# Loads of x in an FFT-mixing and ELU kernel: two-row loads cut in halves, gather lists one a step, the channel matrix in front

## The chip, the cores and the metric

The kernel runs on one core of one Trainium2 chip. The metric is the device time of one execution in microseconds (us), the median of several runs. Five engines work side by side: TensorE (PE; its weight loads are PEld), VectorE (DVE), ScalarE (ACT), GpSimd (POOL) and SyncE (SP), whose queue issues most DMA transfers. The transfers themselves run on 16 DMA engines that all queues share.

## The reference

`x` is 8 batches of 3008 rows and 256 channels. The kernel takes the real part of a 2-D Fourier transform of each batch (along the rows and along the channels) and sends every row through a two-layer network with ELU in between:

```python
def _attn_ref(x):                         # x: (8, 3008, 256) float32
    X = np.fft.fft(x, axis=1)
    X = np.fft.fft(X, axis=2)
    return X.real.astype(np.float32)

def _moe_ref(x, w_in, w_out):             # (24064, 256), (256, 2048), (2048, 256)
    h = x @ w_in
    g = np.where(h > 0.0, h, 1.0 * (np.exp(np.minimum(h, 0.0)) - 1.0))
    return (g @ w_out).astype(np.float32)
```

The weights come as float64, and the kernel converts them itself.

## The kernel before

The transform along the rows uses the symmetries of cosine and sine. The rows of a batch are loaded as four tiles L[0] to L[3] (named `xl` in the profile), two in ascending order (0 and 3, plain loads on the sync queue) and two in descending order (1 and 2, gathers on the GpSimd queue, with row numbers from a small table `ix`). Each partition of a tile holds four rows of one part of the sequence and two rows of another. The tiles are folded (sums e, differences o, then E, O, EO), and the folded tiles are multiplied by the matrices MC. The transform along the channels is folded into the first weight matrix: `fold_chunk` multiplies a converted chunk of `w_in` by the channel matrix CC and gives Wc and Ws.

The loads of one batch:

```python
    def load_x(b):
        L = [
            spool.tile([128, 6 * ND], FP, tag=f"xl{j}", bufs=1, name=f"xl{j}")
            for j in range(4)
        ]
        for j in (2, 1):
            for c, cols in (
                (2 if j == 1 and b == NB - 1 else 0, slice(2 * ND, 6 * ND)),
                (1, slice(0, 2 * ND)),
            ):
                load = nc.gpsimd.indirect_dma_start(
                    out=L[j][:, cols], out_offset=None, in_=xflat,
                    in_offset=bass.IndirectOffsetOnAxis(
                        ap=ix[:, c : c + 1].bitcast(U32), axis=0),
                    element_offset=(b * SEQ + (HALF if j == 1 else 0)) * ND,
                )
                if b == 1:
                    pin(load)
        for j, row in ((3, HALF), (0, 0)):
            nc.sync.dma_start(out=L[j][:, 0 : 4 * ND], in_=xrows(b, row, 4, 128, 4))
            nc.sync.dma_start(
                out=L[j][:, 4 * ND :],
                in_=bass.AP(
                    tensor=xt,
                    offset=x.offset + (b * SEQ + row + 512) * ND,
                    ap=[[2 * ND, 2], [4 * ND, 64], [1, 2 * ND]],
                ),
            )
        ...                                     # one short row of the last batch
        return L
```

`pin` keeps an instruction in program order; instructions without it are placed by a scheduler, which may move them ahead once their tiles are free. `ap` lists step and count of each dimension of the source, slowest first.

The start of the program:

```python
    for _ in range(46):                         # warm-up matmuls on zeros
        mm(idle, zero, zero[:, 0:1].to_broadcast([128, 512]), True)
    exp_neg(warm)
    w1_chunks[0].load()
    L_first = load_x(0)
    nc.sync.dma_start(out=CC, in_=CC_dr.ap())
    load_mats(0, 0, (BE,))
    w1_chunks[1].load()
    nc.sync.dma_start(out=pick, in_=PK_dr.ap())
    ...
    at(-25.0, lambda: fold_now("e3 c3"))        # VectorE folds of the first batch
    at(-24.9, w1_chunks[0].scale)
    at(-24.8, lambda: fold_now("o3 e2 c2 E2 o2 O2"))
    at(-24.5, begin_x_even)                     # xa, xg, xd, xe: read all of L[0..3]
    at(-24.4, lambda: fold_now("e0 c0 e1 c1 E0 EO0"))
    ...
    at(-13.2, lambda: fold_chunk(0))            # first matmuls after the warm-up
    at(-13.1, lambda: dft_now(state["x_even"], 0, "pC"))
    at(-13.0, lambda: dft_now(R_even, 0, "pA"))
```

Everything after that is laid out in steps of `T = 4.8` units of schedule time, 47 steps to a batch. In a step VectorE and ScalarE make the ELU of one block, GpSimd forms four sums of its parts G (for a Strassen-like product) and TensorE multiplies. From batch 2 on GpSimd also folds the next batch's x, one piece in most steps, in 39 of the 47. The loads of the next batch are called once, eight steps before its batch begins:

```python
    for b in range(1, NB):
        s0 = (b - 1) * steps_b
        late = 2 if b == 1 else 0
        l0 = s0 - 8 if b > 1 else 3.2
        at(l0 * T + 0.1, lambda b=b: state.update(L=load_x(b)))
        ...
        def fold_slot(n):
            if b > 1:
                return s0 - 1 + 39 * n // n_big
```

Of the kernel before, what the change touches and what calls it, by code (L numbers as in the profile page):

```python
# [17 lines left out]
SEQ = 3008  # L18
ND = 256
NDFF = 2048  # L20
NF = NDFF // 128
HALF = SEQ // 2
# [85 lines left out]
def kernel(  # L108
# [7 lines left out]
    nc = tc.nc  # L116
    NB = x.shape[0]
# [18 lines left out]
    pin = tc.keep_in_program_order  # L136

    xt = x.tensor

    def xrows(b, row, step, n, rows=6):  # L140

        return bass.AP(
            tensor=xt,
            offset=x.offset + (b * SEQ + row) * ND,
            ap=[[step * ND, n], [1, rows * ND]],
        )
# [23 lines left out]
            )  # L170

    def load_x(b):
        L = [
            spool.tile([128, 6 * ND], FP, tag=f"xl{j}", bufs=1, name=f"xl{j}")
            for j in range(4)
        ]
        for j in (2, 1):
            for c, cols in (
                (2 if j == 1 and b == NB - 1 else 0, slice(2 * ND, 6 * ND)),
                (1, slice(0, 2 * ND)),  # L180
            ):
                load = nc.gpsimd.indirect_dma_start(  # L182
                    out=L[j][:, cols],
                    out_offset=None,
                    in_=xflat,
                    in_offset=bass.IndirectOffsetOnAxis(
                        ap=ix[:, c : c + 1].bitcast(U32), axis=0
                    ),
                    element_offset=(b * SEQ + (HALF if j == 1 else 0)) * ND,
                )  # L190
                if b == 1:
                    pin(load)
        for j, row in ((3, HALF), (0, 0)):
            nc.sync.dma_start(out=L[j][:, 0 : 4 * ND], in_=xrows(b, row, 4, 128, 4))
            nc.sync.dma_start(
                out=L[j][:, 4 * ND :],
                in_=bass.AP(
                    tensor=xt,
                    offset=x.offset + (b * SEQ + row + 512) * ND,
                    ap=[[2 * ND, 2], [4 * ND, 64], [1, 2 * ND]],  # L200
                ),
            )
        if b == NB - 1:
            nc.gpsimd.dma_start(
                out=L[1][0:1, 2 * ND : 5 * ND], in_=xrows(b, SEQ - 3, 1, 1, 3)
            )
        return L


    CC = cpool.tile([128, 384], FP, tag="CC")  # L210
# [10 lines left out]
    class Chunk:  # L221
# [7 lines left out]
        def load(self):  # L229
            dst = self.dst()  # L230
            home = self.home
            if isinstance(home, tuple) and (wide or self.pairs):
                tag, bufs, size = home
                home = spool.tile([128, size], FP, tag=tag, bufs=bufs, name="raw")
            self.ab = home[:, 0:512]
            if not wide:
                nc.sync.dma_start(out=dst, in_=self.src)
                return
            words = home[:, 0:1024].bitcast(I32)
            self.raw = words.rearrange("p (n w) -> p n w", w=2)  # L240
            n = dst.shape[1]
            nc.sync.dma_start(
                out=words.rearrange("p (a b) -> p a b", a=n), in_=self.src.bitcast(I32)
            )
# [137 lines left out]
    def load_mats(ri, kodd, cuts=()):  # L382
        n = (2 * ri + kodd) * BW
        ends = (0, *cuts, BW)
        for a, z in zip(ends, ends[1:]):
            nc.sync.dma_start(
                out=MC[ri, kodd][:, a:z], in_=MC_dr.ap()[:, n + a : n + z]
            )
# [112 lines left out]

    def fold_x(L, engine_of, pieces):

# [254 lines left out]
    def spread_ext(b, kodd):  # L758
        for sl, a, z in ring_cut(b * HALF + kodd * RUN, RUN, False):
            a, z = a + kodd * RUN, z + kodd * RUN  # L760
            nc.sync.dma_start(
                out=Rb[:, sl],
                in_=r128_dr[b : b + 1, a:z].to_broadcast([128, z - a]),
            )
            nc.sync.dma_start(out=Ir[127:128, sl], in_=r128_dr[b : b + 1, a:z])
# [332 lines left out]
    state = {}  # L1098
# [2 lines left out]
        mm(idle, zero, zero[:, 0:1].to_broadcast([128, 512]), True)  # L1101
    exp_neg(warm)
    w1_chunks[0].load()
    L_first = load_x(0)
    nc.sync.dma_start(out=CC, in_=CC_dr.ap())  # L1105
    load_mats(0, 0, (BE,))
    w1_chunks[1].load()
    nc.sync.dma_start(out=pick, in_=PK_dr.ap())
# [16 lines left out]
    def at(t, fn):  # L1125
        events.append((t, len(events), fn))
# [52 lines left out]
    T = PERIOD  # L1179
    for chunk, k in (  # L1180
# [15 lines left out]
        t = k * T  # L1196
# [18 lines left out]
    for c in range(1, 8):  # L1215
        at((2 * c - 2) * T + 4.7 if c > 1 else 2.3, lambda c=c: fold_chunk(c))
        t = (2 * c - 1) * T + 0.03 if c > 1 else 3.0
# [19 lines left out]
    for slot in range(total):  # L1237
        i = slot % 2 * 8 + slot // 2 if slot < 16 else slot
        t = slot * T
# [45 lines left out]
    for q in range(2, n_tiles):  # L1285
        t = (8 * q + 9) * T
# [14 lines left out]
    def safe(col):  # L1301

        return 8 * ((col - 1 - RING) // TW) + 8 if col > RING else 0
# [17 lines left out]
    def at_dft(step, gap, b, ri, kodd, stat):  # L1321
        box = []

        def d():
            if not box:
                box.append(Dft(ri, b, kodd, stat()))
            return box[0]

        at_half(step, d, 0, 0)
        at_half(step + gap, d, 1, b * HALF + (kodd + 1) * RUN)  # L1330

    def begin_folds(b):
        state["EO"], state["ops"] = fold_x(state["L"], lambda key: nc.gpsimd, 2)
# [22 lines left out]
    for n in range(16):  # L1356
        j, k = divmod(n, 4)
# [15 lines left out]
    for b in range(1, NB):  # L1373
        s0 = (b - 1) * steps_b
        late = 2 if b == 1 else 0
        l0 = s0 - 8 if b > 1 else 3.2
        at(l0 * T + 0.1, lambda b=b: state.update(L=load_x(b)))
        first = (6, 7, 7, 8, 9, 9, 10, 10, 12, 15)

        def fold_slot(n):  # L1380
            if b > 1:
                return s0 - 1 + 39 * n // n_big
            return first[n] if n < len(first) else 17 + n - len(first)

        at(fold_slot(0) * T, lambda b=b: begin_folds(b))
        n = 0
        for key in fold_keys:
            slot = fold_slot(n)
            at(
                slot * T + (3.5 if slot < 16 else 1.3),  # L1390
                lambda key=key: state["ops"][key](),
            )
            n += key[0][0] not in "cx"
        for n, (ri, kodd) in enumerate(((0, 0), (1, 0), (0, 1), (1, 1))):
            at_dft(
                s0 + (28, 34 + late, 38 + late, 42 + late)[n], 2, b, ri, kodd,
                lambda k=2 * ri + kodd: state["EO"][k],
            )
        for kodd in range(2):
            step = s0 + (35 if late else 28, 38 + late)[kodd]  # L1400
            assert step >= safe(b * HALF + (kodd + 1) * RUN)
            at(step * T + 1.0, lambda b=b, kodd=kodd: spread_ext(b, kodd))
# [50 lines left out]
```

## Time and profile before

| | |
|---|---|
| time, median of 3 runs | 1982.79 us (1981.92 to 1983.54) |
| span of the profiled execution | 1980.7 us |
| busy: TensorE, GpSimd, VectorE, ScalarE | 1940.8, 1379.1, 1296.3, 864.8 us |
| moved by DMA | 70.25 MB, mean 35 GB/s; 289 GB/s in the first fortieth of the span |
| gathers of x (DMA_INDIRECT on GpSimd) | 32, median 958 ns each on the engine |
| sums of G on GpSimd | 1440, mean 728 ns |
| two-row loads of x | 16, 256 KB each |

In the profile, L414 is the line of all matmuls, L423 that of all GpSimd sums, L182 that of the gathers, L194 and L195 the plain loads of x, L1105 the load of CC. A group is written as line, engine, operation, out<-in. "PE H L414 <- DVE xg L420" reads: a matmul into H waited for VectorE's xg.

### The profile page before, as it was taken

The numbers are of one execution on the slowest core, as the hardware profiler recorded it, in microseconds if no ns is written. First come the engines' busy times: TensorE is split into PE (matmuls) and PEld (weight loads), VectorE is DVE, ScalarE is ACT, GpSimd is POOL, SyncE is SP. The second block draws the span as 40 slices with busy tenths as digits, with TensorE's granted clock in tenths as the row PEclk, the third lists the DMA queues.
The fourth block names the chain that finished last, engine by engine and source line by source line (L and its number), as shares of the span: only waits on it lengthen the run. The fifth ranks groups of instructions, "written<-read, shape, count | busy, mean of one in ns | idle before, by whom it ended". The sixth has DMA issues, their size and how long they took to land.

```text
span 1980.7 us, 27003 instructions
## 1 busy us (share of the span) xinstructions
PE 1940.8 (98%) x8912; PEld 1651.8 (83%) x8912; DVE 1296.3 (65%) x2393; ACT 864.8 (44%) x1669; POOL 1379.1 (70%) x1821
## 2 busy tenths in 40 slices
PE   7999999999999999999999999999999999999998
PEld 4788788888888888888888888888888888888887
DVE  6976666666666666666666666666666666666666
ACT  2654434444344444444444443444444444344443
POOL 2788767786587865777667775678757777455665
PEclk8999999999999999999999999999999999999999
DMA  8235210121011110011101211002010010100101
GB/s 289 80 21 49 60 25 15 36 64 19 13 17 46 48 28 15 18 43 45 27 13 19 59 29 29 11 19 77 18 22 12 19 20 15 18 12 11 22 9 24
DMA packets 263130, 70.25 MB, mean 35 GB/s; under 512 B 248446, under 2 KB 249362, under 8 KB 262992
## 3 DMA queue, kind: packets, MB, share of 16 engines
q1 hardware_dynamic: 257200, 55.69, 14.7%
q0 software_dynamic: 3616, 12.59, 2.0%
q8 instruction: 70, 1.15, 0.3%
q14 instruction: 68, 0.56, 0.1%
q10 hardware_dynamic: 2176, 0.26, 0.1%
HBM read 43.66 MB, written 24.80 MB: 35 GB/s over the span
## 4 chain that ended last, share of the span: by engine, by line
PE 89%; POOL 5%; DVE 3%; issue 1%; SPq 1%; ACT 1%; DMA 0%; DVEq 0%; POOLq 0%; ACTq 0%
PE H L414 36%; PE pB L414 15%; PE pD L414 15%; PE pC L414 15%; PE pA L414 7%; POOL G L423 2%; POOL xl L182 1%; POOL WT L423 1%; DVE E L810 1%; POOL w L423 1%; SPq L1105 0%; DVE G L836 0%; DMA raw<-in_moe_w_in_dram 0%; DVE pow L314 0%; DVE v L420 0%
## 5 line engine op out<-in xcount | busy, mean ns | idle before, releaser
L423 POOL TENSOR_TENSOR G<-G 128x256 f32<-128x256 f32 x1440 | 1034.7, 728 | 528.3 <-DVE G L836 350.4
L810 DVE SCALAR_TENSOR_TENSOR E<-Rb,wex,H 128x256 f32<-128x256 f32 x752 | 328.0, 478 | 582.6 <-PE H L414 577.9
L426 ACT ACTIVATE G<-H 128x512 f32<-128x512 f32 x376 | 224.5, 597 | 974.3 <-DVE G L820 963.7
L414 PE MATMUL H<-Ir,Ws 128*128 128x256 f32 x1504 | 387.1, 380 | 2.7 <-DVE E L810 1.7
L414 PE MATMUL H<-Rr,Wc 128*128 128x256 f32 x1504 | 387.0, 380 | 0.0
L414 PE MATMUL pC<-G,WT 128*128 128x256 f32 x1440 | 369.6, 379 | 1.6 <-DVE u L420 1.6
L414 PEld LDWEIGHTS H<-Rr,Wc 128*128 128x128 f32 x1504 | 284.6, 190 | 56.0 <-issue 3.4
L414 PEld LDWEIGHTS H<-Ir,Ws 128*128 128x128 f32 x1504 | 277.5, 189 | 52.2 <-DVE E L810 4.9
L414 PEld LDWEIGHTS pC<-G,WT 128*128 128x128 f32 x1440 | 273.5, 190 | 39.1 <-issue 2.0
L820 DVE SCALAR_TENSOR_TENSOR G<-E,H 128x512 f32<-128x512 f32 x376 | 256.9, 683 | 48.2 <-POOL G L423 15.2
L836 DVE SCALAR_TENSOR_TENSOR G<-G,H 128x512 f32<-128x512 f32 x376 | 255.7, 680 | 21.6 <-ACT G L426 21.5
L836 DVE SCALAR_TENSOR_TENSOR G<-M,G 128x512 f32<-128x512 f32 x376 | 256.8, 683 | 0.0
L426 ACT ACTIVATE G<-G 128x512 f32<-128x512 f32 x376 | 233.2, 620 | 0.0
L414 PE MATMUL pA<-G,w 128*128 128x256 f32 x784 | 229.3, 379 | 0.6 <-DVE bs L420 0.6
L414 PE MATMUL pD<-G,w 128*128 128x256 f32 x784 | 229.3, 379 | 0.0
L414 PE MATMUL pB<-G,w 128*128 128x256 f32 x784 | 229.3, 379 | 0.0
L414 PE MATMUL pB<-G,WT 128*128 128x256 f32 x720 | 215.7, 381 | 10.4 <-POOL G L423 10.3
L426 ACT ACTIVATE M<-G 128x512 f32<-128x512 f32 x376 | 224.3, 596 | 0.0
L426 ACT ACTIVATE M<-M 128x512 f32<-128x512 f32 x376 | 220.9, 588 | 0.0
L414 PE MATMUL pD<-G,WT 128*128 128x256 f32 x720 | 214.7, 380 | 2.9 <-DVE v L420 2.5
L414 PEld LDWEIGHTS pA<-G,w 128*128 128x128 f32 x784 | 148.9, 190 | 21.1 <-issue 0.9
L414 PEld LDWEIGHTS pD<-G,w 128*128 128x128 f32 x784 | 149.0, 190 | 20.3
(145 smaller groups left out, 1418.2 us busy)
## 6 DMA issues: line engine op xcount, KB each, us to landing
out_dram<-ot SPq DMA_DIRECT2D x496, 32.0 KB
xl<-in_x_dram SPq DMA_DIRECT2D x16, 512.0 KB
xl<-in_x_dram SPq DMA_DIRECT2D x16, 256.0 KB
out_dram<-ot SPq DMA_DIRECT2D x256, 2.0 KB
Rb<-r SPq DMA_DIRECT2D x10, 376.0 KB
raw<-in_moe_w_in_dram SPq DMA_DIRECT2D x7, 512.0 KB
MC<-dft_mats SPq DMA_DIRECT2D x3, 943.5 KB
raw<-in_moe_w_out_dram SPq DMA_DIRECT2D x4, 512.0 KB
```

The source lines that it names most:

```text
L182: load = nc.gpsimd.indirect_dma_start(out=L[j][:, cols], out_offset=None, in_=xflat, in_offset=bass.IndirectOffsetOnAxis(ap=ix[:, c : c + ...
L414: nc.tensor.matmul(out_, lhsT=lhsT, rhs=rhs, start=start, stop=stop, skip_group_check=True)
L423: pin(nc.gpsimd.tensor_tensor(out=o, in0=a, in1=b, op=op))
L426: pin(nc.scalar.activation(out=o, in_=i, func=func, **kw))
L810: nc.vector.scalar_tensor_tensor(out=S.E[:, c], in0=Rb[:, cols(i)], scalar=wex[:, f : f + 1], in1=S.H[:, c], op0=ALU.mult, op1=ALU.add,)
L820: nc.vector.scalar_tensor_tensor(out=two(S.G[:, 0:512])[:, :, ::-1], in0=two(S.E), scalar=2.0, in1=two(S.H), op0=ALU.mult, op1=ALU.subtract,)
L836: nc.vector.scalar_tensor_tensor(out=o, in0=e, scalar=-1.0, in1=h, op0=ALU.add, op1=ALU.max)
```

## The change

It does three things. The load of two rows a partition, one transfer with a three-dimensional source that starts with a dimension of 2, becomes two transfers of 64 partitions each, with plain rows as source. The gathers of tiles 2 and 1 (`back`) become four separate events, all pinned, one a step (for batch 1 one each half step)[...]. And at the start CC is loaded ahead of x instead of behind it. The bytes that are loaded, the folds and the matmuls stay the same.

```diff
     def load_x(b):
+
         L = [ ... ]
-        for j in (2, 1):
-            for c, cols in (
-                (2 if j == 1 and b == NB - 1 else 0, slice(2 * ND, 6 * ND)),
-                (1, slice(0, 2 * ND)),
-            ):
-                load = nc.gpsimd.indirect_dma_start(
+
+        def back(j, few):
+            cols = slice(0, 2 * ND) if few else slice(2 * ND, 6 * ND)
+            c = 1 if few else 2 if j == 1 and b == NB - 1 else 0
+            pin(
+                nc.gpsimd.indirect_dma_start(
                     out=L[j][:, cols],
                     ...
                 )
-                if b == 1:
-                    pin(load)
-        for j, row in ((3, HALF), (0, 0)):
+            )
+            ...                                 # the short row of the last batch
+
+        def ahead(j, row):
             nc.sync.dma_start(out=L[j][:, 0 : 4 * ND], in_=xrows(b, row, 4, 128, 4))
-            nc.sync.dma_start(
-                out=L[j][:, 4 * ND :],
-                in_=bass.AP(
-                    tensor=xt,
-                    offset=x.offset + (b * SEQ + row + 512) * ND,
-                    ap=[[2 * ND, 2], [4 * ND, 64], [1, 2 * ND]],
-                ),
-            )
-        ...
-        return L
+            for half in range(2):
+                nc.sync.dma_start(
+                    out=L[j][64 * half : 64 * half + 64, 4 * ND :],
+                    in_=xrows(b, row + 512 + 2 * half, 4, 64, 2),
+                )
+
+        loads = [lambda n=n: back(2 - n // 2, n % 2) for n in range(4)]
+        return L, loads + [lambda: ahead(3, HALF), lambda: ahead(0, 0)]
@@ start of the program
     w1_chunks[0].load()
-    L_first = load_x(0)
     nc.sync.dma_start(out=CC, in_=CC_dr.ap())
+    L_first, loads = load_x(0)
+    for load in loads:
+        load()
     load_mats(0, 0, (BE,))
@@ later batches
-        l0 = s0 - 8 if b > 1 else 3.2
-        at(l0 * T + 0.1, lambda b=b: state.update(L=load_x(b)))
+        l0, gap = (s0 - 8, 1) if b > 1 else (3.2, 0.5)
+        at(l0 * T + 0.1, lambda b=b: state.update(zip(("L", "loads"), load_x(b))))
+        for n in range(6):
+            t = l0 + gap * n if n < 4 else l0
+            at(t * T + 0.2, lambda n=n: state["loads"][n]())
```

More of the change, by code (lines that the diff above doesn't have):

```diff
@@ L190, in load_x @@
                 )
-                if b == 1:
-                    pin(load)
-        for j, row in ((3, HALF), (0, 0)):
-            nc.sync.dma_start(out=L[j][:, 0 : 4 * ND], in_=xrows(b, row, 4, 128, 4))
-            nc.sync.dma_start(
-                out=L[j][:, 4 * ND :],
-                in_=bass.AP(
-                    tensor=xt,
-                    offset=x.offset + (b * SEQ + row + 512) * ND,
-                    ap=[[2 * ND, 2], [4 * ND, 64], [1, 2 * ND]],
-                ),
-            )
[L203 to L206, printed above, removed]
-        return L
+            )
+            if b == NB - 1 and j == 1 and not few:
+                nc.gpsimd.dma_start(
+                    out=L[1][0:1, 2 * ND : 5 * ND], in_=xrows(b, SEQ - 3, 1, 1, 3)
+                )
+        def ahead(j, row):
+            nc.sync.dma_start(out=L[j][:, 0 : 4 * ND], in_=xrows(b, row, 4, 128, 4))
+            for half in range(2):
+                nc.sync.dma_start(
+                    out=L[j][64 * half : 64 * half + 64, 4 * ND :],
+                    in_=xrows(b, row + 512 + 2 * half, 4, 64, 2),
+                )
+        loads = [lambda n=n: back(2 - n // 2, n % 2) for n in range(4)]
+        return L, loads + [lambda: ahead(3, HALF), lambda: ahead(0, 0)]
     CC = cpool.tile([128, 384], FP, tag="CC")
```

## The prediction

> **What bounds the kernel now.** I read the page first (shares of the engines), then the waits of TensorE, then the chain of waits and the busy time by stretch for the first 30 us, and last the timeline around two of the places where TensorE waits.
>
> ```profile
> PE 1940.8 (98%) x8912; PEld 1651.8 (83%) x8912; DVE 1296.3 (65%) x2393; ACT 864.8 (44%) x1669; POOL 1379.1 (70%) x1821
> ```
>
> TensorE is the bound. Of a span of 1980.7 us it is idle for 39.9 us, and nothing in this change removes a matmul, so 40 us is the most that any change of waits could win. The waits of TensorE over the whole span say where most of that is:
>
> ```profile
> PE H L414 <- DVE xg L420: 11.4, 1, 11.4
> PE pB L414 <- POOL G L423: 10.3, 12, 1.6
> PE pD L414 <- DVE v L420: 2.5, 4, 1.0
> PE H L414 <- POOL raw L423: 2.5, 1, 2.5
> ```
>
> (columns: us in total, times, longest). One wait of 11.4 us at the start, one of 2.5 us behind GpSimd, and twelve of about 1 us behind GpSimd's sums of G. The first one in the chain of waits (start us, us, what):
>
> ```profile
> 3.54 9.74 SPq L1105
> ...
> 18.45 6.33 DMA raw<-in_moe_w_in_dram
> 24.79 0.17 DVE xa L420
> ...
> 25.06 3.68 PE H L414 x16
> ```
>
> L1105 is the load of the channel matrix CC, the sixth load on the sync queue. Its issue takes 9.74 us where its neighbours take about 0.5: the queue stands still until 13.29 us. The second piece is named after a weight load, but the VectorE instruction it ends in (xa) reads only the four x tiles, so the thing that landed last must be x. The busy time by stretch (PE, PEld, DVE, ACT, POOL, PEclk, DMA share, GB/s) shows what the transfers did meanwhile:
>
> ```profile
> 6.00:12.00 6.00, 6.00 (x29) 2.71 (x28) 0.18 (x1) 0.00 (x0) 1.00 (x1) 1.00 0.93 324
> 12.00:13.50 1.50, 1.50 (x8) 0.51 (x6) 0.00 (x0) 0.00 (x0) 0.00 (x0) 1.00 0.18 71
> 13.50:22.00 8.50, 0.11 (x1) 0.00 (x0) 5.71 (x9) 0.51 (x2) 0.00 (x0) 0.65 0.92 274
> 22.00:25.00 3.00, 0.00 (x0) 0.00 (x0) 1.61 (x4) 0.00 (x0) 0.00 (x0) 0.50 0.68 185
> ```
>
> The DMA share falls to 0.18 with most of the program's constants still to be loaded: the queue is stuck behind a transfer that uses few engines. The trace's records of landings confirm it: the semaphore of the first two-row load goes up by fourteen at issue (2.82 us) and by the last two only at 16.01 and 16.05 us, that of the second at 24.54 and 24.66 us. CC, issued by 13.29 us, has fourteen of its sixteen parts by 15.40 us and the last two at 24.92 us. Two DMA engines carry both two-row loads alone, and every later transfer that has a share on those two waits for it.
>
> **What the skill says.** "DMA: Bandwidth & Descriptors", section "Why a DMA increments its semaphore by 16 and not by 1": the number of engines is the largest up to 16 that divides the slowest dimension of both sides, and the unused counts are posted at once. The old source pattern begins with a dimension of 2, which gives 2 engines; the new ones begin with 64 on both sides, which gives 16. The 14 + 2 counts above agree. The same page, section "Queues, rings and completion order": an engine takes its rings in turn, packet by packet, so the GpSimd gathers and the sync loads share the rate; the trace agrees (in 7 to 8 us, 141 KB from one and 217 KB from the other). Its "Rules for kernel authors" advise against splitting a load into partition halves; here the single load was not spread over the engines in the first place, so I do not follow that line. "TensorE: Matmul & The Clock Gate", section "What's actually happening": an idle window drops TensorE to half clock. The trace agrees, with PEclk 0.50 in 22 to 25 us.
>
> **The change part by part.**
>
> (a) *Start: two-row loads on 16 engines, CC in front.* Order on the sync queue: weights chunk 0 (512 KB), CC (192), xl3 (512 + 2 x 128), xl0 (the same), then the matrices. The sync queue also stops being stuck: no engine gets more than its sixteenth. Rates from the records of packets: up to 6.0 us only sync loads move, 1.19 MB in all; afterwards about 400 KB per us, shared with the gathers, 1.5 MB. So chunk 0, CC and the large part of xl3 (1.22 MB) are through at 6.2 us, its two halves (256 KB at 280 and 180 KB/us) at 7.3, and with 0.5 us to landing the first fold (e3) can start at 7.9 instead of 16.15. xl0 follows at 200 KB/us, complete at 11.2; the gathers have L2 at about 11.1 as before, L1 at about 14.5.
> VectorE then: e3, c3, the scaling of chunk 0 and o3 took 3.27 us before (16.15 to 19.42), so e2 at 11.2; e2 to O2 took 4.02 us, so xa at 15.2 where it was 24.79. Then xe and e0 to EO0 took 4.65 us (24.79 to 29.44): done at 19.9. Before, VectorE then lost 1.67 us until 31.11, waiting for a matmul at half clock. Now the fold of chunk 0 can follow the warm-up matmuls (end 13.62) directly, x_even's matmuls run in 15.7 to 17.7, and no wait is left. So the stage that began at 31.11 begins at 19.9: 11.2 us earlier. From there to 60 us VectorE is the bound (9.90 and 9.89 us busy of 10 in 40 to 60 us), and the constants, which move at 400 KB/us behind x, keep ahead (the sine matrix of even k about 20 us, needed about 24). I carry **11.2 us** on.
> A further 0.33 us wait of TensorE at 66.50 us hangs on a 1 KB row (wex) that took from 58.74 to 63.4 us behind batch 1's two-row loads; it goes: **0.3 us**.
>
> (b) *Batch 1's gathers spread.* Now four stand in a row in front of a weight chunk that TensorE needs:
>
> ```profile
> 67.47 0.95 POOL L182 DMA_INDIRECT xl<-in_x_dram,ix  x1 [0.30 <-issue]
> ...
> 68.43 1.27 POOL L423 TENSOR_TENSOR w<-w,pow 128x512 f32<-128x512 f32 x1
> 69.79 2.00 POOL L423 TENSOR_TENSOR raw<-w 128x256 f32<-128x256 f32 x2
> ...
> 71.84 1.08 PE L414 MATMUL H<-raw,CC 128*64 128x256 f32 x8 [2.48 <-POOL raw L423]
> ```
>
> The changed order keeps two of them there and puts two behind: 2 x (0.95 + 0.30) = 2.5 us sooner. GpSimd had 2.9 us of waits in 75 to 82 us (0.82 + 0.69 + 1.38) to take the other two in. Worth **2.5 us**.
>
> (c) *Later gathers, one a step.* Before, they stand in pairs among folds of x:
>
> ```profile
> 416.41 0.98 POOL L182 DMA_INDIRECT xl<-in_x_dram,ix  x1 [0.27 <-POOL o L508]
> ...
> 417.69 0.96 POOL L182 DMA_INDIRECT xl<-in_x_dram,ix  x1 [0.30 <-issue]
> ...
> 418.67 3.03 POOL L423 TENSOR_TENSOR G<-G 128x256 f32<-128x256 f32 x4
> ...
> 420.95 0.70 PE L414 MATMUL pB<-G,WT 128*128 128x256 f32 x2 [0.27 <-POOL G L423]
> ```
>
> One step is 4.75 us (H<-Rr,Wc at 424.07 and 428.82). A step with a pair asks GpSimd for 3.03 (sums) + 1.17 (fold) + 2.5 (pair) = 6.7 us, and the two pairs of a batch end in waits of 0.27 and 1.03 us. The new order has them in steps in which no fold is due: 3.03 + 1.25 = 4.28 us, less than a step. The waits that disappear: 0.88 (at 195.81), 0.27 + 1.03, 0.26 + 1.04, 1.05 + 1.03, 0.85 + 1.03 and 0.28 + 1.03 = **8.75 us**. The gathers come later against the folds, but each tile is first read about ten steps (47 us) after its last list, and the median landing is 4.4 us.
>
> (d) *Added:* 16 more issues on the sync queue, 0.35 to 0.55 us each; the queue has room outside the start.
>
> Sum: 11.2 + 0.3 + 2.5 + 8.75 = 22.75 us. I take off 1.75 us for waits that come up behind the removed ones: 21.
>
> **Rivals.** *The start is given back.* With x early, GpSimd's conversion of weights could bound the stretch 90 to 160 us. For: it is busy 9.70 of 10 us in 90 to 100. Against: TensorE lost only 0.5 us there, and GpSimd's waits are on the other engines, which move earlier as well. If so, some 4 to 6 us of (a) are lost: 1966.
> *The gathers become the bound at the start.* They share the engines with more sync loads than before; if L1 lands at 18 instead of 14.5 us, xa slips by 3 us: 1964.
> *The pairs were not the cause of the waits in (c).* The sums of G also wait for VectorE (350 us in total, but off the path). If the waits stay, (c) is worth nothing: 1970. Against: all ten waits after 300 us sit right behind a pair.
> *Something pinned blocks GpSimd:* a pinned gather that must wait for readers of its tile would hold up the sums. The last readers (o folds) end about fifteen steps before, so I give it little.
>
> **Range and chances.** 1982.8 - 21 = 1961.8, rounded to 1961.5. (a) is uncertain by 3 to 4 us, (c) by 2. Range 1956 to 1968. 2% would be 39.7 us, the whole idle time of TensorE, part of which (the ext stage at 235 to 250 us, 4.5 us) is untouched: faster by over 2% 0.01, within 2% 0.98, slower 0.01.
>
> **What would show it.** (a) the issue of CC and the loads after it each below 1 us; first fold at about 8 us, xa at about 15, no stretch at clock 0.50 before 60 us. (b) no wait of TensorE for raw. (c) no pB wait for POOL after 300 us, gathers single and 4.75 us apart. The prediction is wrong if xa comes after 19 us, or if new TensorE waits add up to over 4 us.

## The result and the profile after

| | before | after |
|---|---|---|
| time, median of 4 runs each, us | 1983.16 (1981.92 to 1983.6) | 1961.07 (1960.25 to 1962.28) |
| ratio | | 0.989, 95% interval 0.9873 to 0.9907 |
| span of the profiled execution, us | 1980.7 | 1958.7 |

The change saves 22.1 us; 21 were predicted. The shares of the engines in the page of the changed kernel:

```profile
PE 1938.8 (99%) x8912; PEld 1652.8 (84%) x8912; DVE 1296.1 (66%) x2393; ACT 864.8 (44%) x1669; POOL 1379.6 (70%) x1821
```

TensorE does the same 8912 matmuls in 2.0 us less of busy time, and its idle time falls from 39.9 to 19.9 us. Where the idle time was is in the waits of TensorE (us in total, times, longest):

```profile
PE pC L414 <- DVE xe L420: 3.1, 1, 3.1
...
PE pD L414 <- POOL G L423: 0.7, 1, 0.7
PE H L414 <- POOL raw L423: 0.6, 1, 0.6
```

The 11.4 us for xg and the twelve waits of pB for G are gone from the list, the wait for raw fell from 2.5 to 0.6, and one wait is new in its place: 0.7 us of pD for G. A wait of 3.1 us for xe stands at the start. The busy time by stretch (PE, PEld, DVE, ACT, POOL, PEclk, DMA share, GB/s), as it was shown of before:

```profile
6.00:12.00 6.00, 6.00 (x29) 2.69 (x28) 1.72 (x4) 0.00 (x0) 0.72 (x1) 1.00 0.99 313
12.00:13.50 1.50, 1.50 (x9) 0.54 (x7) 1.47 (x3) 0.00 (x0) 0.00 (x0) 1.00 1.03 309
13.50:22.00 8.50, 5.39 (x26) 3.33 (x26) 8.22 (x16) 1.48 (x5) 0.00 (x0) 0.84 1.04 380
22.00:25.00 3.00, 3.00 (x11) 1.99 (x11) 2.97 (x6) 0.03 (x1) 0.00 (x0) 0.88 1.04 417
```

The hole in the DMA share (0.18 in 12 to 13.5 us) has closed and VectorE starts earlier. But between 6 and 13.5 us the engines are fully busy at only 310 GB/s, against 417 in the last row, and TensorE still idles 3.1 of the 8.5 us from 13.5 on and falls to half clock for some of it. The chain of waits (start, us, what) no longer has the load of CC in it; it now begins with the four gathers on GpSimd, the last of which lands at 15.93 us:

```profile
4.51 0.95 POOL xl L183
5.46 0.30 issue
5.77 10.16 DMA xl<-in_x_dram,ix
```

That landing releases ScalarE and, through it, later loads on the sync queue; VectorE does not wait for it. VectorE's own list (start, us, instruction, idle time before it) dates the start stage. Before:

```profile
16.15 0.96 DVE L508 TENSOR_TENSOR e<-xl 128x768 f32<-128x768 f32 x1 [9.97 <-DMA xl<-in_x_dram]
...
31.11 0.61 DVE L420 TENSOR_TENSOR bs<-pC,anti 128x189 f32<-128x189 f32 x2 [1.67 <-ACT anti L426]
```

After:

```profile
10.74 0.96 DVE L508 TENSOR_TENSOR e<-xl 128x768 f32<-128x768 f32 x1 [4.25 <-DMA xl<-in_x_dram]
...
14.01 0.95 DVE L508 TENSOR_TENSOR e<-xl 128x768 f32<-128x768 f32 x1
...
17.94 0.16 DVE L420 TENSOR_TENSOR xa<-xl,xl 128x6 f32<-128x6 f32 x1
...
22.50 0.61 DVE L420 TENSOR_TENSOR bs<-pC,anti 128x189 f32<-128x189 f32 x2
```

These are e3, e2, xa and the first bs, which stood at 16.15, 19.42, 24.79 and 31.11 us before. From e3 to bs VectorE now has no idle time, so the stage begins when e3 can begin. bs is 8.6 us earlier. Batch 1's gathers and the matmul that had waited for raw:

```profile
60.71 1.08 PE L414 MATMUL H<-raw,CC 128*64 128x256 f32 x8 [0.56 <-POOL raw L423]
...
62.31 1.01 POOL L183 DMA_INDIRECT xl<-in_x_dram,ix  x1
...
64.80 0.99 POOL L183 DMA_INDIRECT xl<-in_x_dram,ix  x1 [0.16 <-issue]
```

And later gathers, one to a step, with no x fold in between:

```profile
489.46 0.99 POOL L183 DMA_INDIRECT xl<-in_x_dram,ix  x1
490.48 0.73 POOL L423 TENSOR_TENSOR G<-G 128x256 f32<-128x256 f32 x1
...
496.00 0.97 POOL L183 DMA_INDIRECT xl<-in_x_dram,ix  x1
```

Both programs have the same matmuls in the same order, so the start of each can be compared with that of its counterpart. The lead of the changed kernel over the one before changes in these steps (differences of the steady lead on both sides of a place, in the two profiled executions):

| from (us, before) | us gained | what |
|---|---|---|
| 0 to 42 | 8.6 | start stage |
| 66.50 | 0.6 | wait for wex |
| 71.84 | 1.9 | wait for raw |
| 195.81 | 1.2 | wait for G behind a pair |
| 238 to 249.46 | 0.0 | lost 1.42 to a stretch at half clock, got 1.44 back at the wait for G behind it, which that stretch had used up |
| 420.95 to 1400 | 10.5 | ten waits for G behind pairs |
| 1475.87 | -0.9 | new wait for G |

### The profile page after: what moved, and what is told of

The parts are those of the page before. It is cut to its first block, busy times and chain, and to the rows that moved or that the text cites. A ratio compares the mean times of both kernels' runs of the same rounds, so it can differ in the third digit from the quotient of the medians.

```text
span 1958.7 us, 27031 instructions
## 1 busy us (share of the span) xinstructions
PE 1938.8 (99%) x8912; PEld 1652.8 (84%) x8912; DVE 1296.1 (66%) x2393; ACT 864.8 (44%) x1669; POOL 1379.6 (70%) x1821
## 3 DMA queue, kind: packets, MB, share of 16 engines
q1 hardware_dynamic: 257680, 55.69, 15.2%
q8 instruction: 70, 1.15, 0.2%
## 4 chain that ended last, share of the span: by engine, by line
PE 92%; POOL 2%; DVE 2%; DMA 2%; issue 1%; ACT 1%; SPq 0%; DVEq 0%; POOLq 0%; ACTq 0%
PE H L414 37%; PE pD L414 16%; PE pC L414 16%; PE pB L414 16%; PE pA L414 8%; DMA xl<-in_x_dram,ix 1%; DMA raw<-in_moe_w_out_dram 1%; POOL WT L423 1%; POOL w L423 1%; POOL G L423 0%; DMA raw<-in_moe_w_in_dram 0%; DVE E L810 0%; POOL xl L183 0%; DVE G L836 0%; DVE v L420 0%
```

## The experiments

Times are medians; ratios are to runs of the kernel before on the same chip. The diffs are shortened to what matters.

**One part at a time.** The first three kernels are the kernel before with one part of the change each.

*Halves only:*

```diff
-            nc.sync.dma_start(out=L[j][:, 4*ND:], in_=AP([[2*ND, 2], [4*ND, 64], [1, 2*ND]]))
+            for half in range(2):
+                nc.sync.dma_start(out=L[j][64*half : 64*half + 64, 4*ND:],
+                                  in_=xrows(b, row + 512 + 2*half, 4, 64, 2))
```

> The kernel before with the two-row loads cut in halves of 64 partitions, nothing else. Theory (the two-engine loads set the start): about 8.5 to 9.5 us faster than before, some 1974 us; the issue of CC below 1 us, xa at about 17 to 18 us instead of 24.8, and the waits behind the pairs of gathers (8 us in all after 300 us) still there. Rival (the start gained because CC comes first): no more than 2 us faster, 1981 us.

Measured: 1974.21 us, ratio 0.9947 (0.993 to 0.9964), 8.8 us less than before. Its waits of TensorE:

```profile
PE pB L411 <- POOL G L420: 10.3, 12, 1.6
PE H L411 <- POOL raw L420: 3.1, 1, 3.1
PE H L411 <- DMA CC<-chan_mats: 2.8, 1, 2.8
```

The wait for xg is gone and the twelve waits for G all stand. Matmul by matmul the start gains about 10 us, of which some 2 are lost again at 62 us: the wait for raw is longer here (3.1 instead of 2.5 us), and half clock follows it. The new wait for CC (landed at 15.35 us) does no harm, because xa, at 16.66, is what x_even needs. That is 1.3 us earlier than in the changed kernel (17.94), which has CC in front.

*Lists only* (the gathers' instructions on GpSimd, about 1 us each, are called lists): the gathers as four pinned events, one a step; two-row loads and CC as before.

```diff
-        at(l0 * T + 0.1, lambda b=b: state.update(L=load_x(b)))
+        at(l0 * T + 0.1, lambda b=b: state.update(zip(("L", "loads"), load_x(b))))
+        for n in range(6):
+            at((l0 + gap * n if n < 4 else l0) * T + 0.2, lambda n=n: state["loads"][n]())
```

> The kernel before with the gathers pinned one a step, the two-row loads and the place of CC as before. Theory: the shift of TensorE's matmuls grows by 2.0 us at the weight chunk of 72 us and by some 10.5 us behind the places of the former pairs, together 12 to 13.5 us, 1970 us; xa stays at 24.8 us. Rival (the waits belong to VectorE's part of the step): under 4 us, 1979 us or more.

Measured: 1969.83 us, ratio 0.9925 (0.9909 to 0.9942), 13.2 us less. Its waits of TensorE:

```profile
PE H L417 <- DVE xg L423: 12.1, 1, 12.1
...
PE pD L417 <- POOL G L426: 0.7, 1, 0.7
```

The waits of pB for G and of H for raw have left the list, the start has not moved, and the new wait of pD is already here: it belongs to the lists.

*Channel matrix in front only:*

```diff
-    L_first = load_x(0)
     nc.sync.dma_start(out=CC, in_=CC_dr.ap())
+    L_first = load_x(0)
```

> The kernel before with the load of CC in front of x, nothing else. Theory: CC lands by 6 us, but the next load behind x is stuck in its place and x lands as late as before; xa at about 25 us. The fold of the first weight chunk moves into the idle time of TensorE, which frees at most the 1.7 us that VectorE lost at 29.4 to 31.1: 0 to 2 us faster, 1981 to 1983 us. Rival (CC was what held the start): 8 us or more, 1975 us.

Measured: 1984.14 us, ratio 1.0002 (0.9994 to 1.0011): nothing gained. The sync queue's issues show why:

```profile
1.26 0.46 SPq L1104 DMA_DIRECT2D CC<-chan_mats  x1
...
4.34 10.73 SPq L386 DMA_DIRECT2D MC<-dft_mats  x2
```

CC is issued in 0.46 us instead of 9.74, but the standstill has only moved on to the next loads behind the two-row loads, the matrices MC. In both orders the queue stuck at whatever stood behind those loads. The three parts make -8.8, -13.2 and about +1, together -21; all at once give -22.1.

**What made the two-row load slow: few engines, or its size?** In this kernel partition p holds rows 512 + 2p and the next, so that one plain transfer over 128 partitions does it. Tables, constants and the rows written back follow.

```diff
-            for half in range(2):
-                nc.sync.dma_start(out=L[j][64*half : 64*half + 64, 4*ND:],
-                                  in_=xrows(b, row + 512 + 2*half, 4, 64, 2))
+            nc.sync.dma_start(out=L[j][:, 4*ND:], in_=xrows(b, row + 512, 2, 128, 2))
```

> The change as a whole, but the two-row part of every tile now holds rows 512 + 2p in partition p (the tables of row numbers, constants and the rows written back follow), so that it is ONE transfer over 128 partitions instead of two halves of 64. Theory 'engines': the gain at the start came from spreading the two-row transfer over all 16 DMA engines, and the cutting in halves is only one way to do that. Then the time is that of the changed kernel, 1961 us within 1.5 us, e3 starts at 10 to 11 us, and no issue on the sync queue is longer than 1 us. Rival 'halves': a single transfer of two rows a partition is slow in itself, whatever its source pattern. Then e3 starts after 15 us, the sync queue sticks for several us again, and the time is 1968 us or more.

Measured: 1959.57 us (1959.04 to 1961.88; ratio 0.9881, 0.9861 to 0.99) in three runs; a fourth took 2857.44 us at a clock of 0.67 and is not compared. e3 on VectorE:

```profile
9.46 0.96 DVE L505 TENSOR_TENSOR e<-xl 128x768 f32<-128x768 f32 x1 [2.77 <-DMA xl<-in_x_dram]
```

e3 is even a little earlier than expected. A single transfer is as good as two halves once it is spread over all engines, so the old source pattern was the fault and cutting was one cure of two.

**Why the start gained 8.6 and not 11.2 us.** My first idea came from the records of packets: in 7 to 8 us the gathers and the sync loads show about equal numbers of packets (56 and 59), but 225 KB from the gathers' 4 KB pieces and 104 KB from the halves' 2 KB pieces. Then the halves should go ahead of the four-row load, before the gathers begin:

```diff
         def ahead(j, row):
-            nc.sync.dma_start(out=L[j][:, 0:4*ND], in_=xrows(b, row, 4, 128, 4))
             for half in range(2):
                 ...
+            nc.sync.dma_start(out=L[j][:, 0:4*ND], in_=xrows(b, row, 4, 128, 4))
```

> The changed kernel with the two halves of a two-row load issued ahead of the four-row load of the same tile. Theory (DMA engines share by packet, and 2 KB packets beside the gathers' 4 KB ones get a third of the bytes): the 2 KB packets of the first tile are through before the gathers begin at 6 us, the first fold starts at 8 to 8.5 us instead of 10.7 and xa at 16 to 16.5 instead of 17.9; 1.5 us faster than the changed kernel, 1959.5 us. Rival (only the sum of bytes counts): first fold and time unchanged, 1961 us.

Measured: 1961.74 us, ratio 0.9884 (0.9868 to 0.9901), e3 at 12.62 us. A miss: the order inside tile 3 did not help. The gathers' first packet came at 4.35 us in this execution, a microsecond earlier than in the changed kernel (5.34), and the four-row part then stood in the shared time, so the profile does not test the order alone. That left the simpler theory that what counts is how much of tile 3 is through when the gathers begin. To test it the gathers were held back by one fill of a tile on GpSimd:

```diff
+    pin(nc.gpsimd.memset(Rr, 0.0))      # 128 x 2048, only to pass time
     L_first, loads = load_x(0)
```

> The change as a whole, with one extra fill of a 128x2048 tile on GpSimd ahead of the first gathers, which delays them by some 2 us and does nothing else. Theory 'shared engines': the last parts of tile 3 land late in the changed kernel (10.61 us instead of the 7.3 I predicted) because the gathers' packets take their turns on the same DMA engines from 5.7 us on. Then with gathers from 7.7 us on, e3 starts at 8 to 9 us instead of 10.74, and L2 and with it e2 come some 2 us later than before. Rival 'own pace': the two-row halves are slow by themselves (2 KB packets); then e3 stays at 10.5 us or later.

Measured in one execution: 1960.54 us. The gathers' packets begin at about 8 us; e3 and e2 on VectorE:

```profile
9.20 0.96 DVE L508 TENSOR_TENSOR e<-xl 128x768 f32<-128x768 f32 x1 [3.00 <-DMA xl<-in_x_dram]
...
13.94 0.96 DVE L508 TENSOR_TENSOR e<-xl 128x768 f32<-128x768 f32 x1 [1.40 <-DMA xl<-in_x_dram,ix]
```

Now e3 comes 1.5 us earlier (fifteen of the sixteen parts of tile 3 had landed by 7.95 us, the last at 9.07), and e2 waits 1.4 us for tile 2 and starts where it did. xa stays at 17.89. So the gathers did hold tile 3 back, and what tile 3 gained tile 2 paid. The same theory says that fewer bytes in front of tile 3 must help without taking from anyone. Two kernels test it, both with even rows and with the short row moved (below); they differ in one line:

```diff
-    nc.sync.dma_start(out=CC, in_=CC_dr.ap())
     L_first, loads = load_x(0)
     for load in loads[:6]:
         load()
+    nc.sync.dma_start(out=CC, in_=CC_dr.ap())
```

With CC in front:

> As the kernel with even rows, later short row and channel matrix behind x, but with the matrix in front. Theory 'channel matrix in front costs': 1.0 to 1.5 us slower than that one, 1960.7 us, e3 at 9.5 to 10.5 us. Rival 'no difference': within 0.3 us of it, and the first fold differs between executions as much as between the two kernels.

With CC behind x:

> The even rows (two-row part as one transfer over 128 partitions), the short row two steps after the last gather, and the channel matrix BEHIND x again: 1959.5 us. Theory 'channel matrix in front costs': its 196 KB push the end of tile 3 into the time in which the gathers share the engines, so with it behind x e3 starts at 8 to 9 us and xa at 15 to 16.5 us, 1.0 to 1.5 us before the same kernel with the matrix in front. Against it: the fold of chunk 0 then waits for the matrix until about 15 us, which is still ahead of x_even. Rival 'no difference': 0.3 us or less between the two.

Measured: 1958.89 us (1958.04 to 1959.71; ratio 0.988, 0.9863 to 0.9896) with CC in front, 1956.58 us (1956.09 to 1957.32; ratio 0.9869, 0.9853 to 0.9886) behind: 2.3 us, more than expected. In front:

```profile
10.60 0.96 DVE L508 TENSOR_TENSOR e<-xl 128x768 f32<-128x768 f32 x1 [4.61 <-DMA xl<-in_x_dram]
```

Behind:

```profile
6.77 0.96 DVE L508 TENSOR_TENSOR e<-xl 128x768 f32<-128x768 f32 x1 [0.32 <-DMA xl<-in_x_dram]
...
10.80 0.96 DVE L508 TENSOR_TENSOR e<-xl 128x768 f32<-128x768 f32 x1 [0.68 <-DMA xl<-in_x_dram,ix]
...
14.74 0.16 DVE L420 TENSOR_TENSOR xa<-xl,xl 128x6 f32<-128x6 f32 x1
```

192 KB are half a microsecond of transfer at 400 KB/us, but e3 moves by 3.8 us between these two profiles: by the theory, the rest of tile 3 leaves the quick time before the gathers and falls into the shared one. (The first kernel with even rows, also with CC in front, had e3 at 9.46, so part of the 3.8 is chance; the 2.3 us between the times are clear of both ranges.) With CC behind, CC lands at 13.14 us, in time for the fold of chunk 0 behind the warm-up (13.27), TensorE has no wait for xe at all, and the stretches of that kernel show what the changed one missed:

```profile
6.00:12.00 6.00, 6.00 (x29) 2.64 (x28) 4.86 (x8) 0.00 (x0) 0.68 (x1) 1.00 1.01 395
...
13.50:22.00 8.50, 7.73 (x38) 4.99 (x35) 8.26 (x17) 1.52 (x5) 0.00 (x0) 1.00 1.05 407
```

Full clock, and 395 GB/s in 6 to 12 us where the changed kernel has 313. This is the fastest kernel of the study. It beats the change by 4.4 us, which is three steps: the short row moved (1961.02 to 1959.85, last part below), even rows (1959.85 to 1958.89) and CC (1958.89 to 1956.58). The middle step is the least certain, as the ranges of its two kernels overlap.

**Why pairs of gathers made TensorE wait.** The prediction held that a step with sums, a fold and a pair is too full; the rival that the pair itself is at fault. One kernel has pairs in steps without a fold, the other single gathers in steps with one.

```diff
-            t = l0 + gap * n if n < 4 else l0
+            t = l0 + gap * (2 * (n // 2) if b > 1 else n) if n < 4 else l0
```

> The change as a whole, but the four gathers of a batch (batch 2 on) go out in pairs again, two in one step and two in the step after next, in steps in which GpSimd has no fold of x to do. Theory 'overfull step': a wait comes up when sums (3.03 us), fold (1.17) and gathers (1.25 each) of one step exceed the step of 4.75 us by more than the lead GpSimd has. Here 3.03 + 2.5 = 5.53 us, 0.8 us too much, once, with a step of rest behind it: no TensorE wait for G over 0.3 us after 300 us, time 1961 us within 1.5. Rival 'pair': two gathers in a row make TensorE wait whatever else is in the step. Then ten to twelve waits of 0.3 to 1 us are back and the time is 1967 to 1970 us.

Measured: 1962.33 us, ratio 0.9889 (0.9872 to 0.9905). GpSimd's list:

```profile
489.94 0.99 POOL L183 DMA_INDIRECT xl<-in_x_dram,ix  x1
491.23 0.96 POOL L183 DMA_INDIRECT xl<-in_x_dram,ix  x1 [0.30 <-issue]
492.20 0.75 POOL L423 TENSOR_TENSOR G<-G 128x256 f32<-128x256 f32 x1
494.10 3.02 POOL L423 TENSOR_TENSOR G<-G 128x256 f32<-128x256 f32 x4 [1.15 <-PE H L414]
```

The pair is there, and GpSimd is idle for 1.15 us right after it. After 300 us TensorE waits for G only once, at the short row (1.32 us). That and a 0.4 us later start stage are the differences from the changed kernel.

```diff
-            t = l0 + gap * n if n < 4 else l0
+            t = l0 + gap * (n - 13 if b > 2 else n) if n < 4 else l0
```

> The change as a whole, but from batch 3 on the four single gathers go out thirteen steps earlier, in steps in which GpSimd has a fold of x to do. Theory 'overfull step': 3.03 + 1.17 + 1.25 = 5.45 us is 0.7 us more than a step, four times in a row, so GpSimd falls behind by up to 2.8 us, about what it has as a lead: few waits, none over 0.5 us, time 1961 to 1963.5 us. Rival 'pair': a single gather never costs anything: 1961 us, no wait. Rival 'no lead': GpSimd has no lead at all in steps with a fold; then each gather costs TensorE about 0.7 us and the time is 1975 us (20 times 0.7).

Measured: 1964.62 us, ratio 0.9896 (0.9879 to 0.9912). GpSimd's list, first in a usual batch, then in the last one:

```profile
432.16 0.97 POOL L183 DMA_INDIRECT xl<-in_x_dram,ix  x1
433.15 0.74 POOL L423 TENSOR_TENSOR G<-G 128x256 f32<-128x256 f32 x1
433.84 1.00 POOL L508 TENSOR_TENSOR o<-o,o 128x384 f32<-128x384 f32 x1
434.80 2.22 POOL L423 TENSOR_TENSOR G<-G 128x256 f32<-128x256 f32 x3
437.16 0.97 POOL L183 DMA_INDIRECT xl<-in_x_dram,ix  x1
...
1382.14 0.55 POOL L194 DMA_DIRECT2D xl<-in_x_dram  x1 [3.49 <-DMA xl<-in_x_dram,ix]
```

GpSimd works through these steps without a break, one per 5.00 us (432.16 to 437.16), only 0.25 us over a step of 4.75 and not the 0.7 I had expected, and TensorE has no wait for G there. A pair alone is harmless, a single gather beside a fold is harmless; both together, as before the change, made the waits. (The gathers before were also unpinned; pinned pairs beside a fold were not tried.) Most of the time above the changed kernel comes from the last line: GpSimd stands still for 3.49 us, TensorE waits 1.90 us at 1383.50, and the matmuls behind it run at half speed (start, us):

```profile
1384.04 1.85 PE L414 MATMUL H<-MC,e 128*128 128x189 f32 x6
1385.68 1.91 PE L414 MATMUL H<-Rr,Wc 128*128 128x256 f32 x4
...
1389.16 1.03 PE L414 MATMUL H<-Ir,Ws 128*128 128x256 f32 x4
```

One of the four runs took 1960.96 us, the other three 1964.5 to 1965.0; what that one was spared is open, since it has no profile.

**The new wait.** The last batch has one short row that overwrites part of what a gather has just loaded, so it must follow that gather's landing. In the changed kernel it is called right behind the gather, without a pin, and comes ahead of the step's sums:

```profile
1447.40 0.97 POOL L183 DMA_INDIRECT xl<-in_x_dram,ix  x1
...
1452.52 0.55 POOL L194 DMA_DIRECT2D xl<-in_x_dram  x1 [4.15 <-DMA xl<-in_x_dram,ix]
...
1453.07 2.91 POOL L423 TENSOR_TENSOR G<-G 128x256 f32<-128x256 f32 x4
...
1453.88 0.70 PE L414 MATMUL pD<-G,w 128*128 128x256 f32 x2 [0.66 <-POOL G L423]
```

GpSimd sits out the landing (4.15 us), its sums are late, and TensorE waits 0.66 us. In the next kernel the row is an event of its own two steps after the last gather:

```diff
-            if b == NB - 1 and j == 1 and not few:
-                nc.gpsimd.dma_start(out=L[1][0:1, 2*ND : 5*ND], in_=xrows(b, SEQ - 3, 1, 1, 3))
+        if b == NB - 1:
+            at((l0 + 5) * T + 0.2, lambda: state["loads"][6]())    # the same dma_start, pinned
```

> The change as a whole, with the short row of the last batch moved from right behind the gather it depends on to two steps after the last gather, when that gather has long landed. Theory 'pinned behind its gather': GpSimd stood still for 4.15 us at the short row because it waits for that gather's landing; then the wait of TensorE near 1454 us is gone and the time is 0.7 to 0.9 us lower, 1960.2 us. Rival 'wait moves on': the sums are late there for another reason, or the short row blocks wherever it stands; then a wait of 0.5 us or more stays within 30 us of that place and the time is 1961 us.

Measured: 1959.85 us (1959.51 to 1960.82), ratio 0.9886 (0.9869 to 0.9902). The short row in GpSimd's list:

```profile
1465.35 0.54 POOL L196 DMA_DIRECT2D xl<-in_x_dram  x1
```

It waits for nothing, and no wait of TensorE for G is left after 300 us. Against the changed kernel its matmuls gain 0.9 us at that place.

For comparison the changed kernel was run again with these:

> The changed kernel itself once more, as the measure for the three beside it: 1961 us within 1 us. Its new wait of TensorE near 1454 us (0.66 us, pD for GpSimd's G behind the short row) and a first fold e3 between 9.5 and 11 us are expected again.

Measured: 1961.02 us (1960.42 to 1961.65), e3 at 11.51 us, the new wait 0.40 us. The first fold thus varies by about 1 us between executions of the same start (10.74 in the first profile, 11.74 in the kernel with the later short row; 9.46 and 10.60 in the two with even rows and CC in front), so a shift of e3 below that is not read as an effect.

## Why the prediction was right, and where it was not

**(a) Start, predicted 11.2 us, measured 8.6.** This is the mis-sized term. The mechanism held: every sync issue of the first 20 us is below 1 us (one of MC takes 2.76 at 21.04), xl3 and xl0 no longer hang on two engines, and the VectorE durations were right (e3 to e2 3.27 us, e2 to xa 3.93 against the 4.02 I used). What failed is the step "its two halves (256 KB at 280 and 180 KB/us) at 7.3": they had landed at 9.44 and 10.61 us. The engines moved 313 KB/us in 6 to 12 us, not 400 (the line for before already showed 324), and from 6 to 9 us the sync loads had only 88 to 115 KB of each microsecond. My 180 and 200 KB/us for them do not come out of the kernel before either: in 7 to 8 us its packets give 217 KB to the gathers and 141 to the sync loads, and I had let the larger share go to sync. So e3 came 2.8 us late, and e2, xa and bs with it. The late-gather kernel shows that the gathers held tile 3 back, and the two kernels that differ in CC show that moving CC in front, for which I had counted no more than its own 192 KB, costs 2.3 us. My rival of gathers that become the bound had the right pair of transfers, but the wrong one waiting: the loads waited for the gathers. xl0 was later still against its estimate (15.98 us instead of 11.2), but VectorE was busy until xa at 17.94, so this did not show.

Also wrong is "no stretch at clock 0.50 before 60 us": TensorE waits 3.1 us for xe between chunk 0's fold and x_even (clock 0.84 in 13.5 to 22 us). The kernel with even rows and CC behind reaches what I had predicted for the change: e3 at 6.77 (predicted 7.9), xa at 14.74 (15.2), bs at 19.30 (19.9), and full clock in 13.5 to 22 us.

The rival "the start is given back" did not come true: from 42 us to the end the lead shrinks at two places only, by 1.4 us in the half clock near 240 us, got back at once, and by 0.9 at the short row. The 0.3 us for wex became 0.6.

**(b) Predicted 2.5 us, measured 1.9.** The lists alone remove the wait too, the halves alone lengthen it to 3.06. 0.56 us of it are left, so "no wait of TensorE for raw" was too much.

**(c) Predicted 8.75 us, measured 11.7** (1.2 at 195.81 and 10.5 after 300 us). Right in kind, as far as the two kernels on pairs and folds go; too small in size. I had added up the gaps that the list shows. Aligned matmuls gain more at every one: 1.30 where the gap was 1.03, 0.53 where it was 0.26, about 0.27 each. The group right after a gap takes longer (0.70 us for two matmuls that otherwise take 0.59), and the matmul right before it runs its 0.38 us out alone, where the next otherwise starts after 0.22. This is also why TensorE's busy time fell with no matmul removed: by 2.7 us between 300 and 1400 us, against 1.4 us more in the half clock near 240 us. The twelfth wait, at 249.46, was not in my sum, and rightly: without the half clock ahead of it, it is there again (1.57 us in the kernel with pairs in free steps). "Gathers single and 4.75 us apart" was half right: from batch 2 on each is single, but they stand 4.0 to 8.7 us apart.

**(d)** The added issues cost nothing visible, as predicted, though some loads of x took 0.9 to 1.5 us to issue instead of 0.35 to 0.55.

**The 1.75 us taken off** for new waits: one appeared behind GpSimd, 0.66 us in size and 0.9 in effect. It comes nearest to the last rival ("something pinned blocks GpSimd"), which I had given little because I looked for readers of the tile; what blocked was the short row, itself without a pin, which waited for the landing of the gather before.

That the predicted 21 is so close to the measured 22.1 us is therefore luck in part: (a) was 2.6 too high and (c) 2.9 too low, for unrelated reasons.

## What to carry to other kernels

When one issue on a queue takes ten microseconds, look at the transfer ahead of it and at how many engines it is spread over; moving the stuck load only moves the standstill. In a start that is bound by transfers, order by first use, keep out of the way whatever is needed later, and count bytes that share engines with gathers at a fraction of the full rate (here the sync loads had 88 to 115 KB per us in 6 to 9 us). Put side work into steps that have room for the sum of all that is due, and a transfer that depends on another's landing well after it, or the engine that issues it sits the landing out (4.15 us here).

## What I had not expected of the hardware

*Halves move fewer bytes than one transfer of the same size.* In 6 to 12 us, all kernels with two halves moved 301 to 327 GB/s (291 with the gathers held back), and the three with even rows 379, 383 and 395, at about the same busy share (0.94 to 1.04). The Trainium skill, "DMA: Bandwidth & Descriptors", section "Rules for kernel authors", advises one transfer over 128 partitions in place of two halves, a line I had set aside; once the source pattern allowed 16 engines, the runs agree with it. Whether the number of transfers or the 4 KB stride of their rows in memory (even rows lie one after the other) makes the difference was not tried; with even rows the gathers' two-row pieces change their stride as well.

*Half clock after waits is a matter of moment.* The changed kernel and the one with pairs in free steps have the same two waits of TensorE near 226 us (1.6 and 1.0 us). The changed kernel then:

```profile
227.50:231.00 3.50, 2.94 (x7) 2.44 (x8) 1.60 (x3) 1.86 (x4) 2.94 (x5) 0.51 0.42 111
```

The one with pairs:

```profile
227.50:231.00 3.50, 2.52 (x13) 2.25 (x13) 2.54 (x6) 1.56 (x4) 2.53 (x4) 1.00 0.44 111
```

PEclk 0.51 against 1.00. "TensorE: Matmul & The Clock Gate", section "What's actually happening", has the state follow windows of about 3.4 us; the half-clock stretch here is that long. That it depends on how the waits fall into such windows is my reading, not shown.
